# Column 0's transposes copied by ScalarE, the transposes of columns 2 and 3 moved behind all first up halves, one spin less

## Chip, cores, metric

One core of one Trainium2 chip. The metric is the device time of one execution in microseconds (us); lower is better. The experiments ran on three chips: e1 to e4 on one, e5 to e11 on a second, e12 on a third, each with runs of the kernel before on the same chip.

## The reference, cut to what matters

```python
x = A_x                                   # 1 x 2048 x 512, bf16
xn = layernorm(x)                         # over the last axis
out = x + irfft2(rfft2(xn) * (w_r + 1j * w_i)) + (gelu(xn @ w_gate) * (xn @ w_up)) @ w_down
```

The rows of x are taken as 16 "columns" c of 128 rows each (row 16 p + c sits in partition p). The GLU (the last term of `out`) needs xn transposed; the first four columns are transposed on TensorE, the other twelve by DMA.

## The kernel before

The kernel puts every instruction into a list with an estimated duration and dependencies; a list scheduler then fixes the order on each engine. What the change touches is the start-up: two columns are normalised and multiplied first, while the rest is still loading.

```python
for k in range(37):                      # spins: dummy 128x128 matmuls that keep TensorE active
    pin(nc.tensor.matmul(sp_ps[:, :P], lhsT=spin[:], rhs=spin[:], start=True, stop=True))

def spin_on():                           # more of them, between column 0's transposes and the first product
    for k in range(5):
        nc.tensor.matmul(sp_ps[:, :P], lhsT=spin[:], rhs=x_t[:, 0, :P], start=True, stop=True)
...
def first_two():
    ...
    stats(0); mean(0); stats(1)                          # VectorE, in this order
    recip(0); xn_(0, 0); mean(1); xn_(0, 1)
    T(0, 0); T(0, 1)                                     # TensorE: column 0, two transposes each
    add("PE", 0.28, spin_on, [o["T", 0, 1]], key=-1500, lat=0.28, after=o["T", 0, 1])
    table = add("ACT", 1.3, ...Gelu_apprx_tanh..., [o["root", 1]], key=-1500, lat=1.3)   # table load
    v("copy0", lambda: f_Tc(0, 0, 2), 0.25, [("T", 0, 0)], lat=0.4)   # VectorE: PSUM -> xnT
    recip(1)
    v("copy1", lambda: f_Tc(0, 2, 2), 0.25, [("T", 0, 1)], lat=0.4)
    v("xn1", lambda: f_norm_v(1, 0, D), 0.33, [("recip", 1)], lat=0.45)
    ...                                                  # column 1: transposes between gate products
def second_two():                                        # columns 2 and 3: stats, root on GpSimd,
    ...                                                  # scaling on VectorE, 4 transposes each on TensorE
        t = add("PE", 0.23, lambda c=c: f_T(c, 0, NE), [xn_op[c]], key=-880 + c, lat=0.5, acq=("S",))
```

Then TensorE runs 64 gate products (line 502, `g_ps`), 64 up products (`u_ps`), each 128 columns wide, for columns 0 and 1. They come in units of 4 f-blocks (an f-block is 128 of the 1792 hidden features), and each unit is cut over the contraction in two halves of eight products; a "first up half" is the first half of an up unit. Products of two and of four columns follow (line 494).

## Time and profile before

| | |
|---|---|
| Median of the first 3 runs | 178.39 us (178.33 to 178.52) |
| Span of the profiled run | 176.6 us |
| TensorE busy | 171.9 us, 97% of the span |

The page and the chain are quoted in the prediction below. The chain of waits was followed from the instruction that ended last, at each step back to what released it, and is printed in order of time. A line such as "11.39 0.72 PE tp L351 x8" says that from 11.39 us on eight transposes take 0.72 us. In the chain a piece begins where the one before it ended, so its start can lie some 0.2 us after the instruction's own start, which the timeline has (14.34 and 14.18 us for the first two-column gate product).

**S** is the start of the first two-column gate product in the timeline, 14.18 us in the profile before. **G** is the moment from which TensorE's 128-column instructions come 0.056 instead of 0.107 us apart; the trace's clock record begins at that moment where it has such an entry (6.17 us in the profile before). "The clock comes up" means this change of pace and nothing more.

### The profile page before, as it was taken

To read this page: it belongs to the slowest core of one execution; us is meant where nothing else is said; L and a number is where in the kernel's file an instruction comes from. 1 tells how busy PE (TensorE), PEld (TensorE's weight loads), DVE (VectorE), ACT (ScalarE), POOL (GpSimd) and SP (SyncE) were. 2 spreads that over 40 slices of the span, in tenths; PEclk is the share of its full clock that TensorE was granted. 3 is DMA by queue.
4 is the path that set the end of the run, shared out by engine and by line. 5 is a ranking of instruction groups with operands and counts; after the bars stand their busy time and mean duration, and the time that the engine had idled before them with its cause. 6 is when DMAs were issued, how large, how long until landed. Compare 5 with 4: busy or idle time off the path is not lost.

```text
span 176.6 us, 3181 instructions
## 1 busy us (share of the span) xinstructions
PE 171.9 (97%) x1159; PEld 97.5 (55%) x1176; DVE 116.1 (66%) x255; ACT 96.2 (54%) x172; POOL 17.4 (10%) x38
## 2 busy tenths in 40 slices
PE   7999999999999999999999999999999999999993
PEld 7999844555545554555555445454444445444463
DVE  3549999987433699979899999643616325345333
ACT  4552299799646988898899965362112111211200
POOL 1020250504771000000000000000000000000000
PEclk9999999999999999999999999999999999999999
DMA  5999986432825902211211520200122222221212
GB/s 130 340 395 380 324 202 106 94 65 59 230 68 188 344 9 57 59 33 32 59 26 39 142 54 15 59 4 0 59 89 89 85 69 69 79 89 60 84 38 59
DMA packets 20847, 19.35 MB, mean 110 GB/s; under 512 B 8480, under 2 KB 17952, under 8 KB 20832
## 3 DMA queue, kind: packets, MB, share of 16 engines
q1 hardware_dynamic: 20416, 17.84, 34.4%
q0 software_dynamic: 416, 1.32, 2.6%
q8 instruction: 9, 0.15, 0.3%
q14 instruction: 6, 0.05, 0.1%
HBM read 13.38 MB, written 2.10 MB: 88 GB/s over the span
## 4 chain that ended last, share of the span: by engine, by line
PE 97%; issue 1%; DVE 0%
PE y_ps L836 27%; PE g_ps L494 25%; PE u_ps L494 25%; PE sp_ps L320 2%; PE yp L787 2%; PE bp L596 2%; PE g_ps L502 2%; PE gp L757 2%; PE u_ps L502 2%; PE dp L654 2%; PE y_ps L840 2%; PE ep L663 2%; PE tp L351 1%; PE sp_ps L324 0%; DVE y_sb L843 0%
## 5 line engine op out<-in xcount | busy, mean ns | idle before, releaser
L494 PE MATMUL u_ps<-xnT,Wu_sb 128*128 128x512 bf16 (+1 forms) x219 | 52.7, 363 | 0.2
L494 PE MATMUL g_ps<-xnT,Wg_sb 128*128 128x512 bf16 (+1 forms) x217 | 52.4, 363 | 0.4
L836 PE MATMUL y_ps<-Wd_sb,hT 128*128 128x512 bf16 (+2 forms) x247 | 50.5, 355 | 0.2
L512 DVE TENSOR_TENSOR hT<-u_ps,ge 128x512 bf16<-128x512 f32 x56 | 38.1, 688 | 18.2 <-PE u_ps L494 15.4
L507 ACT ACTIVATE ge<-g_ps 128x512 bf16<-128x512 f32 x56 | 33.4, 602 | 22.6 <-PE g_ps L494 19.6
L836 PEld LDWEIGHTS <-hT 128*128 128x128 bf16 x252 | 23.2, 98 | 22.5
L494 PEld LDWEIGHTS <-Wu_sb 128*128 128x128 bf16 x224 | 21.5, 98 | 20.8
L494 PEld LDWEIGHTS <-Wg_sb 128*128 128x128 bf16 x224 | 21.4, 98 | 20.2
L793 ACT CAST yf<-yp 128x512 bf16<-128x512 f32 x16 | 9.3, 586 | 40.5 <-PE yp L787 40.5
L843 DVE TENSOR_TENSOR y_sb<-y_ps,y_sb 128x512 bf16<-128x512 f32 (+2 forms) x18 | 11.1, 631 | 30.0 <-PE y_ps L840 30.0
L668 ACT CAST E<-ep 64x512 bf16<-64x512 f32 x32 | 18.5, 579 | 1.4 <-PE ep L663 1.0
L339 DVE BATCH_NORM_STATS2 stats<-x_t 128x6 f32<-128x512 bf16 x16 | 10.5, 674 | 3.0 <-DMA x_t<-in_A_x_dram 3.0
L456 ACT ACTIVATE xn<-x_t,nb,rstd 128x512 bf16<-128x512 bf16 x12 | 9.5, 814 | 1.0 <-POOL nb L370 1.0
L566 ACT CAST ds<-dp 128x512 bf16<-128x512 f32 x16 | 9.2, 598 | 0.8 <-PE dp L654 0.8
L566 ACT CAST Gs<-gp 128x512 bf16<-128x512 f32 x16 | 8.7, 592 | 0.6 <-PE gp L757 0.5
L566 ACT CAST Bs<-bp 128x512 bf16<-128x512 f32 x16 | 8.5, 611 | 0.5 <-PE u_ps L494 0.5
L799 DVE TENSOR_TENSOR lv<-yf 128x512 bf16<-128x512 bf16 x16 | 6.1, 421 | 1.5 <-ACT yf L793 0.6
L787 PEld LDWEIGHTS <-Gs 128*128 128x128 bf16 x64 | 4.8, 98 | 3.5
L806 DVE TENSOR_TENSOR yt<-lv 128x512 bf16<-128x512 bf16 x16 | 6.1, 422 | 0.3
L787 PE MATMUL yp<-CT,Gs 128*128 128x128 bf16 x64 | 6.0, 219 | 0.1
L840 PE MATMUL y_ps<-yt,RI_t 128*128 128x512 bf16 (+2 forms) x18 | 6.1, 355 | 0.0
L663 PE MATMUL ep<-ds,CT 128*128 128x512 bf16 x16 | 5.7, 379 | 0.0
(68 smaller groups left out, 133.7 us busy)
## 6 DMA issues: line engine op xcount, KB each, us to landing
F<-F SPq DMA_DIRECT2D x32, 64.0 KB, 2.0
y_sb<-in_A_x_dram SPq DMA_DIRECT2D x16, 128.0 KB, 2.1
out_dram<-y_sb SPq DMA_DIRECT2D x15, 128.0 KB, 1.7
x_t<-in_A_x_dram SPq DMA_DIRECT2D x7, 256.0 KB, 8.9
Wd_sb<-in_B_w_down_dram SPq DMA_DIRECT2D x1, 1792.0 KB, 8.6
Wg_sb<-in_B_w_gate_dram SPq DMA_DIRECT2D x2, 512.0 KB, 4.6
Wu_sb<-in_B_w_up_dram SPq DMA_DIRECT2D x2, 512.0 KB, 7.0
Wg_sb<-in_B_w_gate_dram SPq DMA_DIRECT2D x1, 768.0 KB, 10.3
```

What stands on the lines that cost most here:

```text
L339: V.bn_stats(out=st[:], in_=x_t[:, c, :])
L456: xn_op[c] = add("ACT", 0.72, lambda c=c: A.activation(out=xn[:, c, :], in_=x_t[:, c, :], func=AF.Identity, bias=nb[:, c:c + 1], scale=rst ...
L494: T_.matmul(b[name][:, f], lhsT=W_[:, e, (f0 + f) * P:(f0 + f + 1) * P], rhs=rhs[:, e, :], start=(e == 0), stop=(e == NE - 1))
L507: A.activation(out=b["ge"][:], in_=b["g_ps"][:], func=AF.Gelu_apprx_tanh)
L512: V.tensor_tensor(out=hT_of(sb, f0, m, o, w), in0=b["u_ps"][:], in1=b["ge"][:], op=ALU.mult)
L566: A.copy(out=o, in_=i)
L668: A.copy(out=b["E"][64 * h:64 * h + 64, r], in_=b["ep", h][64 * r:64 * r + 64])
L787: T_.matmul(t[:, q], lhsT=late["G"][:, q, c0 + j], rhs=IQ[q], start=(q == 0), stop=(q == 3), skip_group_check=True)
L793: A.copy(out=b["yf"][:, j], in_=b[j][:])
L836: T_.matmul(b[o][:], lhsT=hT_of(sb, f, 1, cl * P, P)[:, 0], rhs=Wd_sb[:, f, o:o + w], start=(f == 0), stop=False)
L840: T_.matmul(b[o][:], lhsT=late["RI"][:, c, :], rhs=late["yt"][:, c, o:o + w], start=False, stop=True)
L843: V.tensor_tensor(out=b["y"][:, o:o + w], in0=b[o][:], in1=b["y"][:, o:o + w], op=ALU.add)
```

## The change

Its intent, in its own words: VectorE scales column 1 sooner because ScalarE copies column 0; the transposes of columns 2 and 3 come behind all first up halves; one spin less. The core of the diff:

```diff
-        for k in range(5):
+        for k in range(4):
...
-        v("copy0", lambda: f_Tc(0, 0, 2), 0.25, [("T", 0, 0)], lat=0.4)
-        o["copy0"].rel = ("S",)
-        xT_op[0, 0] = o["copy0"]
+        xT_op[0, 0], xT_op[0] = (
+            add("ACT", 0.36, lambda h=h: f_Tc(0, 2 * h, 2, A.copy), [o["T", 0, h]], key=-1990 + h, lat=0.48,
+                rel=("S",)) for h in range(2))
         recip(1)
-        v("copy1", lambda: f_Tc(0, 2, 2), 0.25, [("T", 0, 1)], lat=0.4)
-        o["copy1"].rel = ("S",)
-        xT_op[0] = o["copy1"]
...
+            between["t", c] = t
...
+                    if W_ is Wu_sb and k == 3 and i == 0:
+                        between["t", 2].deps.append(o)
+                        between["t", 3].deps.append(o)
```

(The estimated duration of the spins: 0.28 to 0.22.) The prediction calls the three parts (a) moved transposes, (b) one spin less, (c) ScalarE's copies.

More of the change, by code (lines that the diff above doesn't have):

```diff
@@ L410, in first_two @@
         T(0, 1)
-        add("PE", 0.28, spin_on, [o["T", 0, 1]], key=-1500, lat=0.28, after=o["T", 0, 1])
+        add("PE", 0.22, spin_on, [o["T", 0, 1]], key=-1500, lat=0.22, after=o["T", 0, 1])
         table = add("ACT", 1.3, lambda: A.activation(out=warm[:], in_=eps_t[:], func=AF.Gelu_apprx_tanh), [o["root", 1]], key=-1500, lat=1.3)
-        v("copy0", lambda: f_Tc(0, 0, 2), 0.25, [("T", 0, 0)], lat=0.4)
-        o["copy0"].rel = ("S",)
-        xT_op[0, 0] = o["copy0"]
+        xT_op[0, 0], xT_op[0] = (
+            add("ACT", 0.36, lambda h=h: f_Tc(0, 2 * h, 2, A.copy), [o["T", 0, h]], key=-1990 + h, lat=0.48,
+                rel=("S",)) for h in range(2))
         recip(1)
-        v("copy1", lambda: f_Tc(0, 2, 2), 0.25, [("T", 0, 1)], lat=0.4)
-        o["copy1"].rel = ("S",)
-        xT_op[0] = o["copy1"]
         xn_op[0] = o["xn", 0, 1]
```

## The prediction

What the recorded text said of the hardware and no trace of this case shows is cut out of it; the cuts are marked (there is one in the expectation of e6, too). The sum came to 0.27 us for (a), 0.056 for (b) and 0 for (c), together 0.33 us, and so to 178.06 us. I assumed that G stays where it was (6.17 us in the profile before) when a spin is taken out. R1's 179.5 us held more than the 1.2 us of idling (178.06 + 1.2 = 179.26 us). R5 is that G differs from run to run. "The trace has 1.28 us at 5.32" speaks of ScalarE's table load.

> **What bounds the kernel now.** I read the page first for the balance of the engines and the chain that ended last, then the chain in order of time for the first 16 us (the only stretch that the diff touches), then the timeline of that stretch. The page:
>
> ```profile
> PE 171.9 (97%) x1159; PEld 97.5 (55%) x1176; DVE 116.1 (66%) x255; ACT 96.2 (54%) x172; POOL 17.4 (10%) x38
> PE   7999999999999999999999999999999999999993
> PE 97%; issue 1%; DVE 0%
> ```
>
> TensorE is busy in every slice but the first and the last, and the chain that ended last is TensorE for 97% of the span. So time is saved only where TensorE itself waits or does work that is not needed; taking work from VectorE or ScalarE is worth nothing unless TensorE waits for it. Where does it wait? The chain in order of time, from 4 to 16 us (start, length, what):
>
> ```profile
> 5.18 0.48 PE tp L351 x4
> 5.66 0.53 PE sp_ps L324 x5
> 6.19 0.50 PE g_ps L502 x8
> 6.69 0.22 PE tp L351 x4
> 6.92 3.13 PE g_ps L502 x56
> 10.04 1.34 PE u_ps L502 x24
> 11.38 0.01 issue
> 11.39 0.72 PE tp L351 x8
> 12.11 2.23 PE u_ps L502 x40
> 14.34 1.75 PE g_ps L494 x16
> ```
>
> Divide each length by its count. The 56 gate products take 3.13 / 56 = 0.056 us each, the 24 and the 40 up products the same. The five spins take 0.53 / 5 = 0.107 us each, twice as much: they run before the clock has come up. The four transposes of column 1 (at 6.69) take 0.22 / 4 = 0.056 us: no wait. The eight transposes of columns 2 and 3 (at 11.39) take 0.72 us where 8 x 0.056 = 0.45 would do: 0.27 us of waiting sits there. The timeline says for what:
>
> ```profile
> 10.92 0.74 DVE L345 TENSOR_SCALAR xn<-x_t,mv,rstd 128x512 bf16<-128x512 bf16 x2 [1.18 <-POOL rstd L361]
> 11.38 0.55 PEld L351 LDWEIGHTS <-xn 128*128 128x128 bf16 x8 [0.18 <-DVE xn L345]
> 11.39 0.72 PE L351 MATMUL tp<-ident_t,xn 128*128 128x128 bf16 x8
> 11.82 0.58 ACT L354 COPY xnT<-tp 128x512 bf16<-128x512 bf16 x1 [1.02 <-PE tp L351]
> ```
>
> VectorE scales columns 2 and 3 from 10.92 to 11.66 (about 0.33 us apart), because GpSimd gave their factor only then. TensorE had issued its 24th up product at about 11.16 and would have gone on at 11.22; it starts the first transpose at 11.39 (0.17 late) and then waits about 0.10 more for column 3. From 12.11 on I find no wait: the later gaps in the chain are single 512-column products of 0.22 us that lack a record. So the whole removable time is these 0.27 us plus what can be won before 6.2 us.
>
> [...] up products whose operands were there stood 0.27 us behind transposes that were waiting. [...] the trace has 1.28 us at 5.32. That load stands on ScalarE just where the two copies are to go.
>
> **The change part by part.**
>
> (a) Transposes of columns 2 and 3 go behind the first half of the fourth up unit. TensorE then issues 32 up products, then 8 transposes, then 32. Without any lead the first transpose would come at 9.88 + 32 x 0.056 = 11.67 us and the first of column 3 at 11.67 + 4 x 0.056 = 11.89. Column 2 is ready at 10.92 + 0.41 = 11.33, column 3 at 11.66; the page's first transpose began 0.05 us after its data, so they could start at 11.38 and 11.71. Both waits go, with 0.29 and 0.18 us to spare: a gain of 0.27. Is the moved work itself held? The fourth up unit needs the bank that the fourth gelu frees (gelus 8.74 + 2.06 = 10.80); it would start at 9.88 + 24 x 0.056 = 11.22. Not held. What follows the transposes: the two-column gate products, now at 14.18, need the copies of columns 2 and 3. Those copies start some 0.1 to 0.2 us later than now (they end at 12.41 and 12.57), so by 12.8 at the latest, against 13.85 when the gate products are now due. Not held. They also need the first hT product on VectorE, which follows its up product and so moves forward with TensorE.
>
> (b) One spin less. The first gate product starts at 5.99, and 5.45 + 5 x 0.107 = 5.99: exactly when the spins are out. With four it is due at 5.88. [...] what is saved is one instruction at the fast pace: 0.056 us, not 0.107.
>
> (c) Column 0 copied by ScalarE. VectorE's copies take 0.29 and 0.28 us (5.43 and 5.71), ScalarE's copy of the same size, 128x256, takes 0.37:
>
> ```profile
> 5.43 0.29 DVE L354 COPY xnT<-tp 128x256 bf16<-128x256 bf16 x1 [0.22 <-PE tp L351]
> 5.64 0.15 DVE L399 RECIPROCAL rstd<-rstd 128x1 f32<-128x1 f32 x1
> 5.71 0.28 DVE L354 COPY xnT<-tp 128x256 bf16<-128x256 bf16 x1
> 5.91 0.41 DVE L345 TENSOR_SCALAR xn<-x_t,mv,rstd 128x512 bf16<-128x512 bf16 x1
> 6.95 0.37 ACT L354 COPY xnT<-tp 128x256 bf16<-128x256 bf16 x1
> ```
>
> ScalarE is free from 5.30 (its second root), so the first copy runs 5.43 to 5.80; with 0.05 us from data to matmul the first gate product could start at 5.86, just ahead of 5.88. It fits, by 0.02 us. VectorE, without the copies, does the reciprocal at about 5.36 and the scaling at 5.54 to 5.95 instead of 5.91 to 6.32. The transposes of column 1 are due behind eight gate products at 6.53 - 0.056 = 6.47; they would have had their data at 6.32 + 0.05 = 6.37 anyway. So the 0.37 us that VectorE gains buy nothing, and my estimate for (c) by itself is 0, with a risk: the table load moves from 5.32 to about 6.08 and ends at 7.36, the dummy gelu after it at 7.6, the second copy of column 1 at 8.0. TensorE needs that copy for the third unit's second half, about 9.0, and the first real gelu starts at 8.74. About 1 us of slack.
>
> Sum: 0.27 + 0.056 + 0 = 0.33 us. The lead must then live to the end. The up weights land 6.5 us after their issue at 3.21, at 9.7; the first up product would come at 9.82: held by nothing. Later, VectorE and ScalarE are dense between 14 and 45 us, but their work there follows TensorE's products, and the two-column and four-column units of TensorE (0.87 us per four 512-column products) leave them room, since TensorE waits nowhere in that stretch today. So 178.39 - 0.33 = 178.06 us, 0.19% less.
>
> **The rivals.** R1: ScalarE's copy gates TensorE. If it starts later than VectorE's did (the 0.02 us margin of (c)), the first gate product slips by the excess and (b) is lost; worst, if the table load were to run ahead of the copies, they would start at 6.6 and TensorE would idle 1.2 us [...]: 179.5. Against: the copies stand ahead of the table by their key and the root ends well before. R2: the order changes elsewhere. The program order comes from a list scheduler over estimated times, so an earlier column 1 can reorder instructions on any engine up to the end. [...] R3: the lead is taken back at a fixed point, a landing of x or a dense VectorE: the gain falls to about 0.05 and the time is 178.3. Against: no wait of TensorE after 12.1 us. R4: removing a spin saves its full 0.107 us[...]: 178.0. R5: [...] the three runs of before lie within 0.19 us.
>
> **Range and chances.** The main term, 0.27, is a wait seen in the chain and its removal has 0.18 us to spare; I hold it at 85%. The spin's term is 0.05 to 0.11. R1 in its mild form, R2 and R3 move the centre up by a few hundredths, R4 down. Predicted 178.06 us, 8 in 10 between 177.90 and 178.35. To be 2% faster would take 174.8 us, more than TensorE's whole idle time; 2% slower would take 182 us, which only a broken order early on could do. Faster 0.005, within 2% 0.985, slower 0.01.
>
> **What would show it.** In the changed profile the chain should have 32 up products, then eight transposes in about 0.45 us, then 32 up products; four spins of 0.107 us; the first gate product at about 5.88, right behind the spins; eight gate products and column 1's transposes without a gap; VectorE's scaling of column 1 ending about 0.37 us earlier and followed by an idle wait for the transposes; the table load on ScalarE behind two copies, at about 6.1. The first two-column gate product should start near 13.85 instead of 14.18, and every later piece about 0.33 us earlier. I am wrong if ScalarE's copy releases TensorE later than 5.88, if the transposes still wait, or if a new gap shows after 14 us.

## The result and the profile after

Median 177.94 us (177.74 to 178.33, 6 runs) against 178.37 us (178.33 to 178.52, 6 runs). The ratio is 0.9979, 95% interval 0.9966 to 0.9992. A ratio here is the mean time of one kernel's fast runs over the mean of the other's in the same rounds, so it is not quite the ratio of the medians. Executions in which one die ran at a lower clock are left out of the means. (In e9 to e11 ten of the eleven runs of before are those already used for e5 to e8.)

That looks like the prediction come true. The profile does not. It fell on one of the longer of the six runs of the changed kernel, 178.28 us, with a span of 176.6 us as before. The page of the kernel after:

```profile
PE 171.9 (97%) x1158; PEld 97.6 (55%) x1175; DVE 115.7 (66%) x253; ACT 96.8 (55%) x174; POOL 17.4 (10%) x38
...
PE 97%; issue 1%; DVE 0%
```

One matmul less, two VectorE copies less, two ScalarE copies more: the change is all there. Compared instruction by instruction, no engine's order differs anywhere else, so rival R2 is out. The chain of the kernel after, 4 to 16 us:

```profile
5.74 0.43 PE sp_ps L324 x4
6.17 0.78 PE g_ps L500 x8
6.94 0.22 PE tp L351 x4
7.17 3.13 PE g_ps L500 x56
10.29 1.79 PE u_ps L500 x32
12.08 0.45 PE tp L351 x8
12.53 1.79 PE u_ps L500 x32
14.31 1.75 PE g_ps L492 x16
```

The eight transposes take 0.45 us: the wait is gone, and 32 up products stand ahead of them. But the first eight gate products take 0.78 us where before they took 0.50. They ran at 0.107 us apiece nearly to the end: the clock came up at G = 6.73 us, against 6.17 in the profile before. The first gate product itself came at 5.96 us, right behind the spins, not at 5.88, because the first column of x had landed at 3.01 us and not at 2.93. S, before and after:

```profile
14.18 1.91 PE L494 MATMUL g_ps<-xnT,Wg_sb 128*128 128x256 bf16 x16
14.15 1.91 PE L492 MATMUL g_ps<-xnT,Wg_sb 128*128 128x256 bf16 x16
```

S is 0.03 us earlier than before instead of 0.33. On the other engines the timeline of the kernel after has what was foretold:

```profile
5.46 0.69 ACT L354 COPY xnT<-tp 128x256 bf16<-128x256 bf16 x2
5.62 0.41 DVE L345 TENSOR_SCALAR xn<-x_t,mv,rstd 128x512 bf16<-128x512 bf16 x1
6.17 1.28 ACT L412 ACT_TABLE_LOAD   x1
7.09 0.29 DVE L354 COPY xnT<-tp 128x256 bf16<-128x256 bf16 x1 [1.06 <-PE tp L351]
```

ScalarE's two copies stand ahead of the table load; VectorE's scaling of column 1 ends at 6.03 instead of 6.32, and then VectorE idles for 1.06 us until the transposes come. What the copies freed is spent waiting.

From S on, nothing differs. The time from S to TensorE's last matmul is 159.43 us in every trace, and in all but the two with a changed number of loads (e9 and e10) the measured time is S + 164.12 to 164.16. So the question is only what sets S.

### The profile page after: what moved, and what is told of

Its sections match the earlier page's. It is cut to its first block, busy times and chain, and to the rows that moved or that the text cites. A ratio compares the mean times of both kernels' runs of the same rounds, so it can differ in the third digit from the quotient of the medians.

```text
span 176.6 us, 3179 instructions
## 1 busy us (share of the span) xinstructions
PE 171.9 (97%) x1158; PEld 97.6 (55%) x1175; DVE 115.7 (66%) x253; ACT 96.8 (55%) x174; POOL 17.4 (10%) x38
## 4 chain that ended last, share of the span: by engine, by line
PE 97%; issue 1%; DVE 0%
PE y_ps L837 27%; PE g_ps L492 25%; PE u_ps L492 25%; PE sp_ps L320 2%; PE g_ps L500 2%; PE yp L788 2%; PE bp L597 2%; PE u_ps L500 2%; PE gp L758 2%; PE dp L655 2%; PE y_ps L841 2%; PE ep L664 2%; PE tp L351 1%; PE sp_ps L324 0%; DVE y_sb L844 0%
```

## The experiments

Each kernel was built so that every engine's order is that of the kernel before or after apart from the edit named; this was compared instruction by instruction. The exceptions are e7 and its descendants e10 and e12, where the scheduler also swapped a few products and vector operations much later.

### e1: part (a) alone

```diff
+            between["t", c] = t
+                    if W_ is Wu_sb and k == 3 and i == 0:
+                        between["t", 2].deps.append(o)
+                        between["t", 3].deps.append(o)
```

> Only part (a): transposes of columns 2 and 3 behind all four first up halves; VectorE copies and five spins as before; every engine's order is otherwise that of the kernel before. Theory W (the wait for columns 2 and 3 set the time, it ended at a moment fixed by data, and hid when the clock comes up): about 178.0 median, 0.3 to 0.4 under before, and a spread of 0.3 us or more between its runs where before has under 0.2. Theory V (VectorE's earlier scaling of column 1 is what helps, as the change's words say): little of the gain, 178.3.

178.17 us median (177.90 to 178.45), ratio 0.9984 (0.9970 to 0.9998). Between the two theories' figures, with the wide spread that theory W wanted. Its profile had G = 6.93 and S = 14.31, later than before: no gain in that run.

### e2: parts (a) and (b), VectorE copies

The edit of e1, and four spins instead of five.

> Parts (a) and (b): transposes moved, four spins, but column 0 still copied by VectorE. TensorE's order is exactly that of the changed kernel. Theory W: the same time as the changed kernel within 0.1 us, 177.9 to 178.0, since the transposes of column 1 never waited; at most 0.06 us slower in runs where the clock comes up before 5.9 us. Theory V: slower than the changed kernel by 0.1 us or more.

178.39 us median (177.84 to 179.12), ratio 0.9998 (0.9977 to 1.0019). The changed kernel in the same rounds (e4) had 178.32: within 0.1 us, as theory W has it, but the spread is far too wide to prove that on the wall, and both missed the 177.9 to 178.0 that W gave. The trace says more. With VectorE's copies the scaling of column 1 was done at 6.41 us and its transposes were issued at 6.83; they did not wait for it.

### e3: parts (b) and (c) without (a)

The edit of the change without the three lines of (a), and this to keep TensorE's order that of before:

```diff
+                    if W_ is Wu_sb and (k == 3 or i == 1):
+                        o.deps.append(between["t", 3])
```

> Parts (b) and (c) without (a): ScalarE copies column 0, four spins, TensorE's order otherwise that of before (24 up products, eight transposes). Theory W: the lead is used up at the transposes, so 178.35 to 178.4 like before, spread under 0.2 us. Theory V: most of the gain, 178.05.

178.41 us median (178.10 to 178.65), ratio 0.9996 (0.9982 to 1.0010). The median is as theory W expected, and V's gain is not there; but the spread is not under 0.2 us, it is 0.55. The chain of e3 shows why:

```profile
6.09 0.85 PE g_ps L500 x8
6.94 0.35 PE tp L351 x4
...
10.42 1.34 PE u_ps L500 x24
11.76 0.45 PE tp L351 x8
```

This is the old order, 24 up products and then eight transposes, and the transposes take 0.45 us: they do not wait. The clock came up at 7.08 us, TensorE came to them 0.21 us later than in the profile before, and by then columns 2 and 3 were ready. So the wait that (a) removes is not always there.

### e4: the changed kernel again

No edit.

> The changed kernel once more, in the same rounds as its parts. Theory W: 177.74 to 178.33 again, and the profiled run's time goes with the moment at which its clock record begins: about 0.5 us per us of later start beyond 5.9.

178.32 us median (177.99 to 178.41), ratio 0.9993 (0.9980 to 1.0007): in these rounds the gain cannot be told from nothing, and two of the five runs lie above the 178.33 expected. The profiled run was a fast one, 177.99 us, with an early clock (G about 4.8 us). Its chain:

```profile
3.20 6.57 DMA Wu_sb<-in_B_w_up_dram
9.77 0.05 issue
9.82 1.96 PE u_ps L500 x32
11.78 0.45 PE tp L351 x8
```

Here the chain goes back to a DMA. The gate products were done early, and the first up product waited for the first half of the up weights, which landed at 9.77 us: TensorE's instruction came 0.36 us later than the rhythm would have had it. Part of the lead was taken back by a load. S was 13.85 us, just what the prediction had foretold, but for another reason: it counted on a clock that comes up at 6.2 us and on no wait; here the clock came 1.4 us sooner and a load held TensorE. That this number came true is luck.

### What sets S: a sum to be tested

From these traces I formed a new theory. S is the latest of three moments, where g0 is the start of the first gate product, W the landing of the first half of the up weights and X that of columns 2 and 3:

- clock: g0 + 140 x 0.0559 + 0.476 x (G - g0), the last term only if G is later than g0. 140 instructions lie between g0 and S; while the clock is low, one takes 0.107 instead of 0.0559 us, so a share of 1 - 0.0559 / 0.1067 = 0.476 of that time is lost. (The expectations of e5 to e8 have 0.5 for it; e11 has 0.476.)
- up weights: W + 0.05 + 72 x 0.0559 = W + 4.08.
- columns 2 and 3: X + 5.97 in the old order (in the profile before, 14.18 - 8.21), X + 5.5 in the new one, since eight up products fewer stand behind the transposes.

### e5: the changed kernel with one spin in front instead of 37

```diff
-    for k in range(37):
+    for k in range(1):
```

> The changed kernel with 1 instead of 37 spins ahead of the data, so that TensorE's activity begins only with the transposes at 5.0 us and the clock must come up late. Theory C (the time of the changed kernel is set by the moment G at which its clock comes up: the first two-column gate product starts at g0 + 140 x 0.0559 + (G - g0)/2, where g0 is the start of the first gate product, and the time is that start plus 164.13): G between about 8 and 12, so 179.0 to 181.0 us, wide spread, and the profiled run within 0.1 us of the sum. Theory D (the spread is that of the loads' landings, the clock matters little): under 178.5.

179.48 us median (178.90 to 180.00), ratio 1.0057 (1.0031 to 1.0083). G was about 9.3 us, later than in all twelve profiles with the 37 spins in front and the late spins (3.84 to 7.08 us); that it would be late was my assumption until then. The sum gives S = 15.42, measured 15.40; time 179.53 us. Theory C is right, D is out. The chain of e5:

```profile
6.23 0.85 PE g_ps L500 x8
...
7.51 4.04 PE g_ps L500 x56
```

56 gate products take 4.04 us instead of 3.13.

### e6: the changed kernel without late spins

```diff
-        add("PE", 0.22, spin_on, [o["T", 0, 1]], key=-1500, lat=0.22, after=o["T", 0, 1])
```

> The changed kernel without the four spins between the transposes of column 0 and the first gate product. Theory C: the first gate product waits for ScalarE's copy and starts 0.05 us after it, 0.03 to 0.10 earlier than with four spins; worth half of that, so 0.0 to 0.05 us: the same median as the changed kernel within noise. Theory S (these spins are needed to bring the clock up): G later [...] in some runs, time up by 1 us or more in those.

178.09 us median (177.86 to 179.92), ratio 0.9977 (0.9962 to 0.9992). Six of the seven runs lie between 177.86 and 178.31, which is what theory C expected. The seventh, 179.92 us, is the profiled one: G = 9.8 us, later than in all twelve profiles with the late spins and the 37 in front (7.08 at most), and 1.83 us above the median, as theory S has it. In this run x had also landed 0.5 us late, so TensorE stood idle for 0.6 us ahead of the transposes as well. Whether one of the two gaps made the clock late, and which, stays open, and so does whether the late spins guard against it: the changed kernel, which has them, had one run of 180.20 us too (e11).

### e7: first copy on VectorE, second on ScalarE, three late spins

```diff
-        xT_op[0, 0], xT_op[0] = (
-            add("ACT", 0.36, lambda h=h: f_Tc(0, 2 * h, 2, A.copy), ...) for h in range(2))
         recip(1)
+        v("copy0", lambda: f_Tc(0, 0, 2), 0.25, [("T", 0, 0)], lat=0.4)
+        o["copy0"].rel = ("S",)
+        xT_op[0, 0] = o["copy0"]
+        xT_op[0] = add("ACT", 0.36, lambda: f_Tc(0, 2, 2, A.copy), [o["T", 0, 1]], key=-1990, lat=0.48, rel=("S",))
```

> A version meant to beat both: the changed kernel with the first copy of column 0 on VectorE (0.29 us instead of 0.37), the second on ScalarE, the reciprocal of column 1 ahead of the first copy, and three late spins. Theory C: first gate product about 0.1 us earlier, worth 0.05 us when the clock comes up after it, nothing when it comes up before: 177.9 to 178.3 median, not to be told from the changed kernel by the clock on the wall, but by its profile.

178.09 us median (177.89 to 178.30), ratio 0.9980 (0.9966 to 0.9995). In its profile the first gate product came 0.83 us after the first transpose, against 0.94 in the profile of the changed kernel: 0.10 us, about one spin at the slow pace (0.107 us), as expected. On the wall it cannot be told from the changed kernel.

### e8: the kernel before again

No edit.

> The kernel before, run as a kernel of its own, for a second profile of it and for the noise. Theory C: first two-column gate product at the later of (landing of columns 2 and 3) + 5.97 and g0 + 7.83 + (G - g0)/2; median 178.4, ratio 1.000 within the interval.

178.42 us median (178.12 to 178.58), ratio 0.9996 (0.9980 to 1.0011). This is the run that tells most. Its clock came up at 4.07 us, 2.1 us earlier than in the first profile of the same kernel, and yet it took 178.48 us against 178.31. The chain of e8:

```profile
2.69 5.68 DMA x_t<-in_A_x_dram
8.39 1.29 DVE stats L339 x2
...
11.08 0.42 DVE xn L345
11.50 0.05 issue
11.54 0.72 PE tp L351 x8
12.27 2.23 PE u_ps L502 x40
```

The eight transposes take 0.72 us, with the wait, and the chain goes back from them through VectorE's scaling to the load of columns 2 and 3, landed at 8.37 us. 8.37 + 5.97 = 14.34; S was 14.335. (Its first gate product came only at 6.16 us, 0.48 us after the spins, because the gate weights landed at 6.12: one more load that can hold TensorE.) With an early clock the old order is bound by that load; the new order in e4 had S = 13.85.

### e9: the first up weights loaded in two halves

```diff
-        for e in range(0, NE, 2):
-            load_w(T, 0, 1024, e=slice(e, e + 2))
+        for e in (slice(0, 2), slice(2, 4)) if T is Wg_sb else (slice(0, 1), slice(1, 2), slice(2, 4)):
+            load_w(T, 0, 1024, e=e)
```

> The changed kernel with the first 0.5 MB of the up weights loaded as two halves, so that the first half lands sooner; every compute engine's order unchanged. Theory L (when the clock comes up early, the changed kernel waits for this load, 0.36 us in the early run seen so far): no wait or one under 0.2 us at the first up product in a run with an early clock, so the fastest runs are 0.1 to 0.2 us faster than the changed kernel's; nothing in runs with a late clock; the median 0.0 to 0.1 us lower, inside the noise.

178.73 us median (178.34 to 178.92), ratio 1.0013 (0.9997 to 1.0030): a miss, slower than the changed kernel. S was 14.13, exactly the clock's sum for G = 6.56. But the time was S + 164.57, not S + 164.13. The 0.44 us are at the end of the program, see e12. The clock came up too late for the load's wait to be tested here.

### e10: e7 and e9 together

> The split copy of column 0 with three late spins, and the split load of the up weights. Theories C and L together: 0.05 us lower with a late clock, 0.1 to 0.2 with an early one; median 177.8 to 178.2, ratio to before about 0.998.

178.37 us median (178.16 to 178.63), ratio 0.9998 (0.9983 to 1.0013): a miss for the same reason. The clock was early (3.84 us) and the idea worked: the first up product started at 9.65, with one wait of 0.09 us for the second half where e4 had waited 0.36; S was 13.77. The time was S + 164.59.

### e11: the changed kernel as control

No edit.

> The changed kernel as the control of the two before it, in the same rounds: median 177.9 to 178.3. Its profiled run again fits the sum: first two-column gate product at the latest of g0 + 7.83 + 0.476 x (G - g0), the landing of the first up weights + 4.08, and the landing of columns 2 and 3 + 5.5; time = that + 164.13.

178.18 us median (177.98 to 180.20), ratio 1.0010 (0.9973 to 1.0046); one run at 180.20 us, without a profile. The profiled run (178.09 us) fits: early clock, columns 2 and 3 landed late at 8.44, so 8.44 + 5.5 = 13.94 is the latest moment; S was 13.96.

### e12: e10 with the number of loads restored

```diff
-    for c in range(0, NC, 8):
-        nc.sync.dma_start(out=RF_t[:, c:c + 8], in_=rf_d.rearrange("p (c k) -> p c k", c=NC)[:, c:c + 8])
+    nc.sync.dma_start(out=RF_t[:], in_=rf_d.rearrange("p (c k) -> p c k", c=NC))
```

> The kernel of e10 with the two loads of RF_t made one, so that the number of loads and stores is again that of the changed kernel; all compute engines' orders are those of e10. Theory E (the 0.44 us that e9 and e10 lost lie after the last store: the closing waits take the eight DMA semaphores in a fixed order, and one load more puts the last store on the first of them, so that seven more waits of some 65 ns follow its landing): the time is again the start of the first two-column gate product + 164.13, median 177.8 to 178.0, ratio to before about 0.997, and faster than the changed kernel's 178.0 to 178.2. Theory F (the split load itself costs, by the DMA engines' work): 178.3 as e10.

178.19 us median (177.78 to 178.29), ratio 0.9984 (0.9970 to 0.9998). Profiled: S = 13.78, time 177.94 us = S + 164.16. The 0.44 us are back, so theory E is right and the split load is innocent. The waits of SyncE after 172 us, for the changed kernel:

```profile
SPq L896 <- DMA out_dram<-y_sb: 0.7, 2, 0.4
```

and for e10:

```profile
SPq L897 <- DMA out_dram<-y_sb: 1.1, 1, 1.1
```

The program ends with SyncE waiting on eight DMA semaphores one after the other. In the changed kernel the last store is on the last of them: two waits, and when the store lands all is done. In e10 it is on the first: one long wait, and seven more checks of 59 to 70 ns (0.44 us) follow it in the trace. As for beating the changed kernel: e12's median of 178.19 is not below that kernel's 178.18 over all its 17 runs, and the two did not share rounds; it also missed the 177.8 to 178.0 expected. By its profile it removes two waits; by the wall it is the same.

### The profiled runs beside the sum

| Run | order | g0 | G | latest moment | S by the sum | S measured | time |
|---|---|---|---|---|---|---|---|
| before | old | 5.99 | 6.17 | columns 2 and 3 | 14.18 (taken from it) | 14.18 | 178.31 |
| e8, before again | old | 6.16 | 4.07 | columns 2 and 3 | 14.34 | 14.34 | 178.48 |
| e3, (b)(c) | old | 5.88 | 7.08 | clock | 14.28 | 14.28 | 178.41 |
| after | new | 5.96 | 6.73 | clock | 14.15 | 14.15 | 178.28 |
| e4, after | new | 5.67 | 4.8 | up weights | 13.85 | 13.85 | 177.99 |
| e11, after | new | 5.94 | 4.7 | columns 2 and 3 | 13.94 | 13.96 | 178.09 |
| e1, (a) | new | 6.08 | 6.93 | clock | 14.31 | 14.31 | 178.43 |
| e2, (a)(b) | new | 5.97 | 7.04 | clock | 14.31 | 14.30 | 178.44 |
| e5, 1 spin | new | 6.02 | 9.3 | clock | 15.42 | 15.40 | 179.53 |
| e7, split copy | new | 5.94 | 6.70 | clock | 14.13 | 14.13 | 178.28 |
| e6, no late spin | new | 6.38 | 9.8 | clock | 15.84 | 15.79 | 179.92 |

The sum was formed on the profiles of before, after and e1 to e4; e5 to e8 and e11 test it. e9, e10 and e12 load the up weights in halves and stand in their own sections: the clock's moment is 14.13, 13.69 and 13.79 us there, and S was 14.13, 13.77 (with the wait of 0.09) and 13.78.

The landings and moments are the trace's own records; in e4, e5, e6 and e11, whose clock record is empty, G is the first 128-column instruction at the fast pace.

## Why the prediction was right, and where it was not

The measured 177.94 us lies in the range and near the 178.06 foretold, and the mechanism of the main term is right. But the working treats as fixed two things that move from run to run, so the agreement is partly luck of the first six runs.

**Step (a), 0.27 us.** Right in kind. "A wait seen in the chain and its removal has 0.18 us to spare": in every profile of the new order but one the eight transposes take 0.45 us (e11, with a late load, 0.62). As to size, it is a gain that depends on the clock. With an early clock it was larger than foretold: S was 14.34 in e8 and 13.85 in e4, a difference of 0.48 us. Of this 0.19 us is only that columns 2 and 3 landed later in e8 (8.37 against 8.18); with the same landing some 0.30 us would be left. With the clock at 7.08 it is zero, for the wait is not there (e3). Around G = 6.2, the case the prediction was worked out on, the sum gives 13.9 for the new order and 14.18 for the old: 0.28.

**Step (b), 0.056 us.** Supported by the sum, not measured by itself, and only if G stays where it is. By the sum, 0.107 us less in g0 is worth 0.107 x (1 - 0.476) = 0.056 us when the clock rises after g0, and the sum fits the clock-limited traces of the table, whose g0 lie between 5.88 and 6.38, to 0.05 us. When the clock is up before and a load or the copy decides, it is worth nothing by the sum: loads set S in e4 (13.85), e8 (14.34) and e11 (13.96), and ScalarE's copy held the first gate product of e11 by 0.08 us. On the wall, e2 with one spin less was 0.22 us slower than e1 in the same rounds, which is the spread and not the spin. Rival R4, that a spin less saves its full 0.107 us, was not tested.

**Step (c), 0.** Supported for a late clock: VectorE's earlier scaling bought an idle wait of 1.06 us in the profile after, and in e2 column 1's transposes did not wait with VectorE's copies either. The runs on the wall (e2 178.39, e4 178.32, in the same rounds) cannot tell 0 from 0.1. The change's own reason, "so that VectorE scales column 1 sooner", is not where its gain comes from. With an early clock no run tests (c): in e4 the transposes of column 1 were issued at 6.11 us, while in e8, with VectorE's copies, the scaling ended at 6.21. Without ScalarE's copies TensorE might have waited some 0.1 us there (my estimate), which the later wait of 0.36 us for the up weights would have swallowed. The mild form of R1 is real with an early clock: in e11 the first gate product stood 0.08 us behind the spins, waiting for ScalarE's copy, which ended at 5.89 us. (In e4 it stood 0.08 us behind them too, but there the gate weights landed at 5.61 us, together with the end of the copy.)

**The step that failed is "the lead must then live to the end ... held by nothing".** In e4 the first up product was held 0.36 us by the up weights, landed at 9.77, although the prediction had looked at exactly that landing. It was checked for the one clock of the one profile, where 0.1 us was to spare. R3, the lead taken back at a fixed point, was listed and dismissed because "no wait of TensorE after 12.1 us" is seen; the wait is before 12.1. One smaller reading was wrong, without consequence: the 3.6 us of a gain of 2% are not "more than TensorE's whole idle time", which the page puts at 176.6 - 171.9 = 4.7 us.

**R5, that G differs from run to run, was dismissed on a wrong argument.** "The three runs of before lie within 0.19 us" was taken as a sign that the clock is steady. The old order hides the clock: whether it came up at 4.07 or 6.17 us, S was set by the load of columns 2 and 3 (14.34 and 14.18 us). Nor does the clock come up at a fixed time, as the 0.056 us of step (b) took it to: in the twelve profiles with all 37 spins in front and late spins too, G lies between 3.84 and 7.08 us. What sets it within that range is not shown. Over all rounds 45 runs of before range from 178.03 to 179.01, and 17 of after from 177.74 to 178.41 with one at 180.20; medians 178.42 and 178.18. My own follow-up, that the old order keeps its spread under 0.2 us, fell too (e3, and before itself in later rounds): its load also lands at different moments (8.18 us in e4, 8.51 in the profile after). Even a landing at 8.5 gives no more than 178.6 us by the sum; the runs of before from 178.68 to 179.01 had no profile and stay unexplained.

So the gain is real but small and uneven: by the sum, about 0.3 us if the clock is up by some 6.2 us, shrinking to 0.06 us if it comes up past 7. The ratio that a handful of runs shows (0.9979, then 0.9993 and 1.0010; the last is 0.9987 without the run of 180.20) probably depends on which clocks they drew, but only the profiled runs show their clock. What stays open: the runs of 179.12 (e2) and 180.20 us (e11) had no profile. By the sum they would need a G near 8.5 and 10.8 us, or a late first gate product as well, like e6; this is argued, not shown.

## What to carry to other kernels

A wait that sits at the end of a start-up can hide all jitter (differences from run to run) ahead of it; remove it and the next bound shows, here a clock (G from 3.84 to 7.08 us) and a load (landed at 8.18 us in e4, at 8.51 in the profile after) that differ from run to run. So ask of every wait not only what it costs in this profile but what would be the bound without it, and profile the same kernel several times before believing a margin of 0.1 us. When a small edit adds or removes a DMA, compare the time after the last store too: the closing waits may cost more than the edit saves (0.44 us in e10, more than the wait of 0.36 us that the edit was to remove).
